# Dilated attention and a mixture of experts on one Trainium2 core: three matmuls of zeros at the start, and a straight run over all tile slots with the check at the end

## The chip, the cores and the metric

The kernel runs on one core of one Trainium2 chip. The core has a matrix engine (TensorE: PE, with its weight loads shown as PEld), a vector engine (VectorE: DVE), a scalar engine (ScalarE: ACT), GpSimd (POOL) and SyncE (SP), which issues most of the DMA transfers. The metric is device microseconds (us) of one execution; lower is better. A program is measured several times, and the median is given.

## The reference

The input is a batch of 8 sequences of 576 positions with 8 heads of 64 features. The first four heads attend to a window of 32 positions, the other four to every fourth position of a window of 128. The result, 4608 tokens of 512 features, goes to a layer of 8 experts in which every token has exactly one expert, its own best one or the one of the token before it:

```python
logits = np.einsum('bsd,de->bse', x, w_gate)
local_gate = 1.0 / (1.0 + np.exp(-np.einsum('bsd,de->bse', x, w_local).squeeze(-1)))
for b in range(B):
    prev_e = -1
    for s in range(S):
        fresh_e = int(np.argmax(logits[b, s]))
        if s == 0 or local_gate[b, s] < 0.5:
            e = fresh_e
        else:
            e = prev_e if prev_e >= 0 else fresh_e
        prev_e = e
        p = softmax(logits[b, s])
        h = np.maximum(x[b, s] @ w1[e], 0.0)
        out[b, s] = p[e] * (h @ w2[e])
```

`w1[e]` is 512 x 1024 and `w2[e]` is 1024 x 512. Everything is float32.

## The kernel before

`whole` holds the computation. It is called once with `exact=False`, and under a branch a second time with `exact=True`. In the fast version the exponentials of the attention are taken without subtracting a maximum, so a check of the sums of exponentials is needed: `check` (L683) tests whether all reciprocals of sums, kept in `rec`, lie within bounds, adds the answers up with one matmul over the partitions (`all`, L692), and writes one integer, `bad` (L693). If it is set, the branch at L168 runs the exact version over the same inputs. Both versions stand in the program; with these inputs only the fast one is executed.

**The attention stage.** The loop at L625 runs over 32 units of two heads. For each unit, `load` (L211) issues on SP the transfers of `kq` (592 KB) and `vt` (438.8 KB), two units ahead; `kq` has two buffers, `vt` three. `scores` (L250) makes 18 small matmuls into `sc` (36 instructions in the trace, since every float32 matmul appears there as two), DVE applies the mask (L266), ACT takes the exponential (L269), `values` (L302) multiplies by `vt` into `pv`, and after every second unit `turn` (L321) transposes the result with 128x128 matmuls (L332). Between the units the routing of finished quarters of the batch is fed in piece by piece by `gap` (L614): logits, choice of the expert, and `place` (L458), which scatters one row of a table `tab` in DRAM for each token with twelve indirect DMAs of GpSimd.

**The tile slots.** The tokens are grouped by expert into tiles of 128. With 4608 tokens and 8 experts there can be at most NT = 43 tiles; how many are really filled depends on the inputs. The kernel has 43 slots, numbered t. A slot without tokens has expert 7 (the number is clamped), the token number 4608, whose row in `xd` is zero, and for the output an address outside of `out_dram`, which the scatter drops. `expert(t)` (L661) is one slot:

- `hidden` (L589), twice: 32 instructions each on PE (L596), the rectifier on ACT (L598);
- `weights(t + 2, ...)` (L565): SP loads the expert's number into a register and issues the transfer of `w1s` (2048 KB) and later of `w2s` (2048 KB), with the condition that the expert differs from the one two slots before, since there are two buffers of each;
- `features(t + 1)` (L581): four transposes on PE (L585) and a copy on DVE (L587), one for each slot;
- `gather(t + 3)` (L574): two indirect DMAs of GpSimd;
- `output` (L600): 16 instructions on PE (L604), scaling on DVE (L606), scatter on GpSimd (L607).

**What sets the order.** PE runs in the order in which the program text issues its work (`manual_schedule`); the other engines' order is left to the framework. All matmul results share four PSUM banks (`bank`, L199). Slots 0 to 39 (LAST = 40) stand in line. After slot 18, `check` is issued, and its answer is loaded into a register of every engine (`register`, L680). After slot 36, `number`, the count of filled tiles that `table(True)` wrote at L513, is loaded in the same way. Slots 40 to 42 stand behind a branch on that number (L703), and then comes the branch on `bad` (L168):

```python
for t in range(LAST):
    expert(t)
    if t == CAP // 2 and not exact:
        again = check()
    if t == CAP:
        number = register(tiles["number"], NT, "a sum of tiles")
with tc.If(number > LAST):
    for t in range(LAST, NT):
        expert(t)
```

Of the kernel before, what the change touches and what calls it, by code (L numbers as in the profile page):

```python
# [10 lines left out]
F32 = mybir.dt.float32  # L11
BF16 = mybir.dt.bfloat16
I32 = mybir.dt.int32
U16 = mybir.dt.uint16
Act = mybir.ActivationFunctionType
Alu = mybir.AluOpType
# [6 lines left out]
P = 128  # L23
B, H, S, DH = 8, 8, 576, 64
D = H * DH
E, F = 8, 1024
# [33 lines left out]
CAP = N // P  # L60
NT = CAP + E - 1
# [6 lines left out]
EARLY, FIRST = 2, 11  # L68

KEPT = EARLY * GB * 2  # L70
assert EARLY * GS - E * (P - 1) > (FIRST - 1) * P

LAST = CAP + E // 2


FRESH = -(2.0 ** -23)
# [66 lines left out]
@with_exitstack  # L143
def dilated_attn_locality_moe_kernel(
    ctx: ExitStack,
    tc: tile.TileContext,
    qk: bass.AP,
    v: bass.AP,
    wgl: bass.AP,
    w1: bass.AP,  # L150
    w2: bass.AP,
    con: bass.AP,
    msk: bass.AP,
    qmk: bass.AP,
    out: bass.AP,
):
    nc = tc.nc
    keep = ctx.enter_context(tc.tile_pool(name="keep", bufs=1))
    cst = keep.tile([P, C_ALL], F32, name="cst")
    wg = keep.tile([P, DK, LW], F32, name="wg")  # L160
    ones = keep.tile([P, P], F32, name="ones")
    bad = keep.tile([1, 1], I32, name="bad")
    nc.vector.memset(ones, 1.0)

    args = (qk, v, wgl, w1, w2, con, msk, qmk, out, cst, wg, ones)
    again = whole(tc, False, bad, *args)

    with tc.If(again > 0):  # L168
        whole(tc, True, bad, *args)

# [2 lines left out]
def whole(ctx, tc, exact, bad, qk, v, wgl, w1, w2, con, msk, qmk, out, cst, wg, ones):  # L173
    nc = tc.nc
    name = "exact" if exact else "plain"
# [3 lines left out]
    def pool(name, bufs, **kw):  # L179
        return ctx.enter_context(tc.tile_pool(name=name, bufs=bufs, **kw))  # L180
# [7 lines left out]
    once = pool("once", 1)  # L188
# [10 lines left out]
    def bank(shape, name):  # L199
        return banks.tile(shape, F32, name=name, tag="bank")  # L200
# [10 lines left out]
    def load(n):  # L211
        kq = ins.tile([P, WIN + 2 * S], F32, name="kq", bufs=2)
        vt = ins.tile([KW, 2, NB, VW], F32, name="vt")
        nc.sync.dma_start(out=kq, in_=qk[n])
        nc.sync.dma_start(out=vt.rearrange("p u i e -> p (u i e)"), in_=v[n])
        loaded[n] = kq[:, :WIN + S], kq[:, WIN + S:], vt

    load(0)
    if not exact:
        mk = once.tile([KW, 2 * S], BF16, name="mk")  # L220
# [262 lines left out]
    tiles, stage = {}, {False: once}  # L483

    def table(late):
        nt = NT - FIRST if late else FIRST
        w = "late" if late else "early"

        def new(shape, name, dtype=F32):
            return stage[late].tile(shape, dtype, name=f"{name}_{w}")  # L490

        cn = bank([P, E], "cn")
        nc.tensor.matmul(cn, lhsT=ones[:TB], rhs=routes[NG - 1 if late else EARLY - 1]["cum"][:, :, NJ],
                         start=True, stop=True)
        ni = new([P, E], "ni", I32)
        nc.vector.tensor_scalar(ni, cn, float(P - 1) if late else 0.0, None, Alu.add)
        nc.vector.tensor_scalar(ni, ni, 7, None, Alu.logical_shift_right)
        nf = new([P, E], "nf")
        nc.vector.tensor_copy(nf, ni)
        if late:  # L500
            nc.vector.tensor_tensor(nf, nf, tiles["done"], op=Alu.subtract)
        end = new([P, E], "end")
        nc.vector.tensor_tensor_scan(end, nf, nf, 0.0, Alu.add, Alu.max)
        if not late:

            done = new([P, E], "done")
            nc.vector.tensor_tensor(done, nf, end, op=Alu.subtract)
            nc.vector.tensor_scalar(done, done, float(FIRST), 0.0, Alu.add, Alu.max)
            nc.vector.tensor_tensor(done, done, nf, op=Alu.min)
            tiles["done"] = done  # L510
        else:
            tiles["number"] = new([1, 1], "number", I32)
            nc.vector.tensor_scalar(tiles["number"], end[0:1, E - 1:], float(FIRST), None, Alu.add)  # L513
        ge = new([1, nt, E], "ge")
        shape = [1, nt, E]
        nc.vector.tensor_tensor(ge, end[0:1].unsqueeze(1).to_broadcast(shape),
                                cst[0:1, C_ROW:C_ROW + nt].unsqueeze(2).to_broadcast(shape), op=Alu.is_le)
        er = new([1, nt], "er")
        nc.vector.tensor_reduce(er, ge, axis=AX.X, op=Alu.add)
        tiles["experts", late] = experts = new([1, nt], "experts", I32)  # L520
        nc.vector.tensor_scalar(experts, er, float(E - 1), None, Alu.min)

        gc = new([nt, E], "gc")
        nc.vector.tensor_scalar(gc, end[:nt], cst[:nt, C_COL:C_PAY], None, Alu.is_le)
        ec = new([nt, 1], "ec")
        nc.vector.tensor_reduce(ec, gc, axis=AX.X, op=Alu.add)
        nc.vector.tensor_tensor(gc, gc, end[:nt], op=Alu.mult)
        at = new([nt, 1], "start")
        nc.vector.tensor_reduce(at, gc, axis=AX.X, op=Alu.max)
        nc.vector.tensor_tensor(at, cst[:nt, C_COL:C_PAY], at, op=Alu.subtract)  # L530
        nc.vector.scalar_tensor_tensor(at, ec, float(CAP), at, Alu.mult, Alu.add)
        if late:
            of = new([nt, E], "of")
            nc.vector.tensor_scalar(of, cst[:nt, C_IDX:C_REV], ec, None, Alu.is_equal)
            nc.vector.tensor_tensor(of, of, tiles["done"][:nt], op=Alu.mult)
            nc.vector.tensor_reduce(ec, of, axis=AX.X, op=Alu.add)
            nc.vector.tensor_tensor(at, at, ec, op=Alu.add)
        ri = new([nt, 1], "ri", I32)
        nc.vector.tensor_scalar(ri, at, float(PADS), None, Alu.min)
        tiles["rows", late] = tr = new([nt, P, TW], "tr")  # L540
        i = nc.gpsimd.indirect_dma_start(
            out=tr.rearrange("t s c -> t (s c)"), out_offset=None, in_=tab.rearrange("(r s) c -> r (s c)", s=P),
            in_offset=bass.IndirectOffsetOnAxis(ap=ri, axis=0))
        for s in scatters:
            tc.add_manual_dep(i.ins, s.ins.name, SYNC, reason="all places")
        table_users.append(i)
# [34 lines left out]
    def features(t):  # L581
        x = xg.pop(t).rearrange("p g f -> p (g f)")
        tp = bank([P, DK, P], "tp")
        for kk in range(DK):
            nc.tensor.transpose(tp[:, kk], x[:, kk * P:(kk + 1) * P], ident)  # L585
        xe[t] = mp.tile([P, DK, P], F32, name="xe")
        nc.vector.tensor_copy(xe[t], tp)  # L587
# [26 lines left out]
    def gap():  # L614
        if waiting:
            waiting.pop(0)()
# [41 lines left out]
        weights(t, True)  # L658

    features(0)  # L660
    def expert(t):  # L661
        if t == FIRST - 3:
            assert not waiting
            tokens(True)
        hidden(t, 0)
        gap()
        hidden(t, 1)
        gap()
        if t + 2 < NT:
            weights(t + 2, False)  # L670
        if t + 1 < NT:
            features(t + 1)
        if t + 3 < NT:
            gather(t + 3)
        output(t)
        gap()
        if t + 2 < NT:
            weights(t + 2, True)

    def register(value, most, why):  # L680
        return nc.values_load(value, min_val=0, max_val=most, skip_runtime_bounds_check_because=why)  # L681

    def check():  # L683

        flat = rec.rearrange("p n i -> p (n i)")
        fine = once.tile([P, NPB * NB], F32, name="fine")
        nc.vector.tensor_scalar(fine, flat, 1.0 / HIGH, None, Alu.is_ge)
        nc.vector.scalar_tensor_tensor(fine, flat, 1.0 / LOW, fine, Alu.is_le, Alu.mult)
        least = once.tile([P, 1], F32, name="least")
        nc.vector.tensor_reduce(least, fine, axis=AX.X, op=Alu.add)  # L690
        lp = bank([1, 1], "all")
        nc.tensor.matmul(lp, lhsT=least, rhs=ones[:, 0:1], start=True, stop=True)  # L692
        nc.vector.tensor_scalar(bad, lp, float(P * NPB * NB), None, Alu.is_lt)  # L693
        return register(bad[0:1, 0:1], 1, "a comparison's result")

    again = None
    for t in range(LAST):
        expert(t)
        if t == CAP // 2 and not exact:
            again = check()  # L700
        if t == CAP:
            number = register(tiles["number"], NT, "a sum of tiles")
    with tc.If(number > LAST):  # L703
        for t in range(LAST, NT):
            expert(t)
    return again

# [48 lines left out]
```

## Time before and its profile

| | |
|---|---|
| median of 3 runs | 842.93 us (841.5 to 846.79) |
| the profiled execution | 846.79 us, of which the trace's span is 845.0 us |
| PE busy (share of the span) | 776.0 us (92%), 6000 instructions |
| PEld busy | 593.9 us (70%) |
| DVE, ACT, POOL busy | 167.1 us, 117.5 us, 171.3 us |
| DMA | 179.60 MB, mean 213 GB/s |
| first instruction of L596, last scatter (L607) issued | 238.2 us, 830.5 us |

The page of a profile gives the busy time of each engine, the span in 40 equal slices with the busy share of each engine in tenths (here one slice is 21.1 us), the groups of instructions by line with their count, their total and mean duration and the idle time before them, and what ended that idle time. "PEclk" is the clock that TensorE was granted, in tenths of full speed. The timeline lists instructions in order of time, with adjacent ones of one kind merged; "idle before <-releaser" tells how long the engine sat idle before it, and what ended that. A "q" behind an engine's name means its sequencer, which handles registers, branches, semaphores and the issue of DMAs.

### The profile page before, as it was taken

How to read it: one execution, taken by the hardware profiler on the slowest of the kernel's cores; microseconds unless marked ns; L12 is line 12 of the kernel's file. 1: busy time of each engine (PE TensorE's matmuls, PEld its weight loads, DVE VectorE, ACT ScalarE, POOL GpSimd, SP SyncE). 2: the span in 40 equal slices, each digit the busy share in tenths (PEclk: the TensorE clock that was granted, in tenths of full speed). 3: DMA queues.
4: the chain of work that ended last, by engine and by line, in shares of the span. 5: the costliest groups of instructions: out<-in, count | busy, mean ns of one | idle time of the engine just before them, and what ended most of it. 6: DMA issues, size and time to landing. Idle time of an engine off the chain costs nothing. (4 is left out here: it accounts for less than half of the span.)

```text
span 845.0 us, 14238 instructions
## 1 busy us (share of the span) xinstructions
PE 776.0 (92%) x6000; PEld 593.9 (70%) x6000; DVE 167.1 (20%) x450; ACT 117.5 (14%) x201; POOL 171.3 (20%) x184
## 2 busy tenths in 40 slices
PE   6899698796779899999999999999999999999992
PEld 6878677675567577768686776768686767777770
DVE  3445254253312211110111111110011111111110
ACT  2342232232200000100000000101000000001010
POOL 1001303204042531121212121111212121212110
PEclk9985595578689999999999999999999999999997
DMA  8996685688948698989656571688118484282110
GB/s 284 254 260 183 133 253 141 186 263 227 318 140 304 195 365 322 332 318 330 243 211 251 192 279 38 236 321 327 40 38 310 152 295 171 70 324 104 35 39 16
DMA packets 44557, 179.60 MB, mean 213 GB/s; under 512 B 6403, under 2 KB 24963, under 8 KB 37568
## 3 DMA queue, kind: packets, MB, share of 16 engines
q1 hardware_dynamic: 35312, 157.06, 56.3%
q0 software_dynamic: 9168, 21.48, 7.4%
q8 instruction: 52, 0.85, 0.4%
q14 instruction: 25, 0.20, 0.1%
HBM read 230.28 MB, written 20.59 MB: 297 GB/s over the span
## 5 line engine op out<-in xcount | busy, mean ns | idle before, releaser
L596 PEld LDWEIGHTS hp<-xe,w1s 128*128 128x128 f32 x2560 | 294.2, 193 | 20.0 <-issue 17.9
L596 PE MATMUL hp<-xe,w1s 128*128 128x128 f32 x2560 | 295.5, 276 | 2.7 <-DVE bad L693 1.5
L604 PE MATMUL yp<-w2s,h 128*128 128x512 f32 x640 | 283.2, 595 | 3.9 <-issue 3.9
L604 PEld LDWEIGHTS yp<-w2s,h 128*128 128x128 f32 x640 | 119.0, 191 | 139.3 <-issue 139.3
L598 ACT ACTIVATE h<-hp 128x512 f32<-128x512 f32 x80 | 47.8, 597 | 541.6 <-PE hp L596 528.5
L261 PE MATMUL sc<-kq 64*96 64x64 f32 x1152 | 81.2, 308 | 17.0 <-issue 8.3
L261 PEld LDWEIGHTS sc<-kq 64*96 64x96 f32 x1152 | 75.5, 218 | 24.9 <-issue 14.1
L577 POOL DMA_INDIRECT xg<-xd,tok x43 | 41.8, 973 | 228.6 <-PE tp L585 150.7
L607 POOL DMA_INDIRECT out_dram<-y,tok x40 | 40.3, 1007 | 230.5 <-DVE y L606 193.4
L587 DVE COPY xe<-tp 128x512 f32<-128x512 f32 x41 | 28.3, 691 | 267.9 <-PE tp L585 259.8
L474 POOL DMA_INDIRECT tab<-cst,pi x48 | 44.0, 917 | 173.4 <-DVE pi L472 113.4
L606 DVE TENSOR_SCALAR y<-yp,gate 128x512 f32<-128x512 f32 x40 | 30.0, 751 | 244.9 <-PE yp L604 244.9
L312 PE MATMUL pv<-vt,pr 96*64 96x65 f32 x1152 | 62.7, 282 | 15.6 <-issue 15.6
L266 DVE SCALAR_TENSOR_TENSOR pr<-sc,mk 96x640 f32<-96x640 f32 x64 | 48.1, 753 | 114.3 <-PE sc L261 43.1
L312 PEld LDWEIGHTS pv<-vt,pr 96*64 96x64 f32 x1152 | 55.8, 191 | 20.2 <-issue 17.7
L269 ACT ACTIVATE pr<-pr 96x640 f32<-96x640 f32 x64 | 43.6, 684 | 132.0 <-DVE pr L266 127.8
L577 POOL DMA_INDIRECT xg<-xd,pos x43 | 40.8, 950 | 13.1 <-issue 11.9
L332 PE MATMUL tp<-cst,x 128*128 128x128 f32 x144 | 30.9, 379 | 5.9 <-issue 2.8
L332 PEld LDWEIGHTS tp<-cst,x 128*128 128x128 f32 x144 | 24.0, 197 | 9.3 <-issue 4.0
L585 PE MATMUL tp<-cst,xg 128*128 128x128 f32 x164 | 25.4, 277 | 3.8 <-DMA xg<-xd,tok 3.8
L317 DVE TENSOR_TENSOR x<-pv,rec 128x320 f32<-128x320 f32 x64 | 26.1, 447 | 0.1
L335 ACT COPY xt<-tp 128x384 f32<-128x384 f32 x48 | 22.9, 500 | 19.5 <-PE tp L332 10.4
(120 smaller groups left out, 111.6 us busy)
## 6 DMA issues: line engine op xcount, KB each, us to landing
w1s<-in_w_dram SPq DMA_DIRECT2D x44, 2048.0 KB
w2s<-in_w_dram SPq DMA_DIRECT2D x44, 2048.0 KB
kq<-in_qk_dram SPq DMA_DIRECT2D x32, 592.0 KB
vt<-in_v_dram SPq DMA_DIRECT2D x32, 438.8 KB
xd<-x SPq DMA_DIRECT2D x32, 288.0 KB
tab<-cst,pi POOLq DMA_INDIRECT x48
xg<-xd,tok POOLq DMA_INDIRECT x43
xg<-xd,pos POOLq DMA_INDIRECT x43
```

The costliest lines, as they stand in the source:

```text
L261: nc.tensor.matmul(sc[:KW, u, (i - a) * QB:(i - a + 1) * QB], lhsT=kt[h, i * QB:i * QB + KW], rhs=qt[h, i * QB:(i + 1) * QB], start=True, ...
L266: nc.vector.scalar_tensor_tensor(pr[:, :, :w], sc[:KW, :, :w], -CEIL, mk[:, at:at + w].unsqueeze(1).to_broadcast([KW, 2, w]), Alu.max, Alu ...
L269: nc.scalar.activation(pr[:, :, :w], pr[:, :, :w], Act.Exp, scale=SCALE)
L312: nc.tensor.matmul(pv[u * QB:(u + 1) * QB, i - a], lhsT=pr[:, u, (i - a) * QB:(i - a + 1) * QB], rhs=vt[:, u, i], start=True, stop=True, t ...
L332: nc.tensor.transpose(tp[:, i].rearrange("p u q -> p (u q)"), x[:, c * w + i].rearrange("p g d -> p (g d)"), ident)
L474: i = nc.gpsimd.indirect_dma_start(out=tab, out_offset=bass.IndirectOffsetOnAxis(ap=pi[:, j:j + 1], axis=0), in_=pay[:, g, j], in_offset=None)
L577: nc.gpsimd.indirect_dma_start(out=x[:, g], out_offset=None, in_=xd[g] if t >= FIRST else xd[g][:EARLY * GS], in_offset=bass.IndirectOffse ...
L596: nc.tensor.matmul(hp[:, m], lhsT=w1s[t % 2][:, half * FK // 2 + m, kk], rhs=x[:, kk], start=(kk == 0), stop=(kk == DK - 1))
L598: nc.scalar.activation(ht[t][:, half * FK // 2:(half + 1) * FK // 2], hp, Act.Relu)
L604: nc.tensor.matmul(yp, lhsT=h[:, m], rhs=w2s[t % 2][:, m], start=(m == 0), stop=(m == FK - 1))
L606: nc.vector.tensor_scalar(y, yp, of_tile("gate", t), None, Alu.mult)
L607: nc.gpsimd.indirect_dma_start(out=out, out_offset=bass.IndirectOffsetOnAxis(ap=of_tile("tok", t), axis=0), in_=y, in_offset=None, bounds_ ...
```

## The change

Four things are edited. Before the first load, DVE writes zeros into a tile `blank` of 128x512, and three matmuls of it with itself (128x128 by 128x512, float32) go into a PSUM bank `idle` that nobody reads. The branch at L703, the constant LAST, and the count `number` (L513 and its register loads) are gone: the loop runs over all 43 slots. The check is issued after the last slot in place of after slot 18. And the register load of `bad` stands in the calling function, behind all of it. The exact version has no check and no matmuls of zeros.

```diff
-    again = whole(tc, False, bad, *args)
+    whole(tc, False, bad, *args)
+    again = nc.values_load(bad[0:1, 0:1], min_val=0, max_val=1,
+                           skip_runtime_bounds_check_because="a comparison's result")
     with tc.If(again > 0):
         whole(tc, True, bad, *args)
...
+    if not exact:
+        blank = once.tile([P, 512], F32, name="blank")
+        nc.vector.memset(blank, 0.0)
+        idle = bank([P, 512], "idle")
+        for i in range(3):
+            nc.tensor.matmul(idle, lhsT=blank[:, :P], rhs=blank, start=True, stop=True, skip_group_check=True)
     load(0)
...
-        else:
-            tiles["number"] = new([1, 1], "number", I32)
-            nc.vector.tensor_scalar(tiles["number"], end[0:1, E - 1:], float(FIRST), None, Alu.add)
...
-    def expert(t):
+    for t in range(NT):
...
-    def check():
+    if not exact:
         flat = rec.rearrange("p n i -> p (n i)")
...
         nc.vector.tensor_scalar(bad, lp, float(P * NPB * NB), None, Alu.is_lt)
-        return register(bad[0:1, 0:1], 1, "a comparison's result")
-
-    again = None
-    for t in range(LAST):
-        expert(t)
-        if t == CAP // 2 and not exact:
-            again = check()
-        if t == CAP:
-            number = register(tiles["number"], NT, "a sum of tiles")
-    with tc.If(number > LAST):
-        for t in range(LAST, NT):
-            expert(t)
-    return again
```

On the engines: PE starts with the three matmuls and ends with slot 42, the matmul of the check and the register load of `bad`. DVE has the 128x512 memset third in its queue, ahead of the memsets of `fill`; its three large instructions of the check (L687 to L690) stay where they were, early in the program, and only the one that writes `bad` comes last, behind the scaling of slot 42. GpSimd issues 43 scatters in place of 40; the 43 pairs of gathers were issued before too.

## The prediction

> **What bounds the kernel now.** I read the page first, then the groups by line, then the timeline at each place that the change touches.
>
> ```profile
> span 845.0 us, 14238 instructions
> PE 776.0 (92%) x6000; PEld 593.9 (70%) x6000; DVE 167.1 (20%) x450; ACT 117.5 (14%) x201; POOL 171.3 (20%) x184
> PEclk9985595578689999999999999999999999999997
> DMA  8996685688948698989656571688118484282110
> L596 PE MATMUL hp<-xe,w1s 128*128 128x128 f32 x2560 | 295.5, 276 | 2.7 <-DVE bad L693 1.5
> L604 PE MATMUL yp<-w2s,h 128*128 128x512 f32 x640 | 283.2, 595 | 3.9 <-issue 3.9
> ```
>
> PE is the bound: 92% busy, and from about 290 us on at full clock almost without a gap. The counts matter most. A slot has 64 instructions of L596 and 16 of L604; 2560 / 64 = 40 and 640 / 16 = 40. So 40 slots were executed and the branch at L703 passed over slots 40 to 42: they are not in the 845.0 us.
>
> What is a slot worth? The copy of L587 occurs once in each slot, behind its transposes on PE, so its starts in the timeline of DVE are the clock of the loop:
>
> ```profile
> 517.28 0.69 DVE L587 COPY xe<-tp 128x512 f32<-128x512 f32 x1 [6.83 <-PE tp L585]
> 533.55 0.69 DVE L587 COPY xe<-tp 128x512 f32<-128x512 f32 x1 [8.59 <-PE tp L585]
> 548.00 0.69 DVE L587 COPY xe<-tp 128x512 f32<-128x512 f32 x1 [6.83 <-PE tp L585]
> ...
> 808.10 0.69 DVE L587 COPY xe<-tp 128x512 f32<-128x512 f32 x1 [6.83 <-PE tp L585]
> 822.55 0.69 DVE L587 COPY xe<-tp 128x512 f32<-128x512 f32 x1 [6.83 <-PE tp L585]
> ```
>
> The step is 14.45 us from 533.55 to the end (14.45 x 20 = 289.0 = 822.55 - 533.55). Only the step before it is 16.27 us, and there the check stands, as the timeline at 524 us shows:
>
> ```profile
> 524.04 0.19 PE L692 MATMUL all<-ones,least 128*1 128x1 f32 x2
> 524.82 0.14 DVE L693 TENSOR_SCALAR bad<-all 1x1 int32<-1x1 f32 x1
> 525.69 7.38 PE L596 MATMUL hp<-xe,w1s 128*128 128x128 f32 x64 [1.46 <-DVE bad L693]
> ```
>
> PE's queue holds the register load of `bad` ahead of slot 19, so it stood until DVE, behind the scaling of slot 18, had written the answer.
>
> The start, in the timeline of PE: 36 score matmuls take 3.14 us at first, and 1.75 us from 27.74 us on.
>
> ```profile
> 4.65 3.14 PE L261 MATMUL sc<-kq 64*96 64x64 f32 x36 [4.65 <-DMA kq<-in_qk_dram]
> ...
> 27.74 1.75 PE L261 MATMUL sc<-kq 64*96 64x64 f32 x36
> ...
> 36.57 1.89 PE L261 MATMUL sc<-kq 64*96 64x64 f32 x36 [1.37 <-DMA kq<-in_qk_dram]
> ```
>
> **What the Trainium skill says.** "TensorE: Matmul & The Clock Gate", section "What's actually happening": TensorE runs at half clock until it has been busy for a window of about 3.4 us, and falls back after an idle one. The trace agrees on the factor (3.14 against 1.75 us) but not on the time: PE was busy without a break from 15.18 to 27.74 us before the small score matmuls ran fast, and windows of 1 us over the first slot, whose full-width matmuls start at 236.05 us, show the clock rise at about 242.9 us, after 6.8 us.
>
> "Runtime: NRT & Kernel Launch", section "Instruction fetch mechanics": a taken branch to code that is not in the fetched pages waits for a fetch. The trace agrees: at L168, which jumps over the whole exact version, PE's branch took 3.34 us, and GpSimd's next instruction came 3.4 us after its branch. "VectorE: DVE Perf Modes", section "Zero memsets can be issued as uint32", gives one cycle per element for a memset; the trace has its own number, 1.02 us for 128x1152 (L232).
>
> **The change part by part.**
>
> *Three more slots.* Each has all the instructions of a filled one; that its tokens are missing takes none away. On PE, 3 x 14.45 = +43.35 us. Everything else lies beside that, as it does now: per slot 1.19 us of ACT, 1.44 us of DVE, 2.9 us of GpSimd. Would an empty slot wait for data? The gathers of slots 40 to 42 were issued already (43 pairs of L577 for 40 slots) and nothing waited. Its expert is 7; the last expert has five tiles, slots 35 to 39, so both weight buffers hold expert 7 by slot 36, and the conditional loads of slots 40 to 42 move nothing. DMA is nearly still in the last slices ("2110"). Without that cover: two matrices of 2048 KB at the 321 GB/s of the window from 360 to 400 us take 13 us, still less than a slot; a step of 15.56 us at 357 to 373 us shows what a tight load costs, +1.1 each, 3.3 for all. I take 43.35, with 42.5 to 46.7 as bounds.
>
> *The check out of the middle.* 16.27 - 14.45 = -1.82 us on PE. The three large DVE instructions stay early, off the path. The load of `number` on PE at 779.9 us goes too, worth nothing: the steps around it are 14.45. Next after the wait comes slot 19, whose data was there. `number`'s 0.14 us on DVE (L513) goes as well.
>
> *The end.* From the scaling of slot 39 (829.42) to the end are 15.6 us. GpSimd is last through it, as the lines for L703, L681, L168 and L754 show (min/median/max ns, first and last start):
>
> ```profile
> L703 POOLq INC_SWDGE_SEM  x1: 1395/1395/1395, 831.5 to 831.5; - x1
> L681 POOLq TENSOR_LOAD <-bad x1: 308/308/308, 832.9 to 832.9; - x1
> L168 POOLq COMPARE_BRANCH  x1: 45/45/45, 833.3 to 833.3; - x1
> L168 POOLq EVENT_SEMAPHORE  x5: 17/43/43, 836.7 to 837.1; - x5
> L168 POOLq INC_SWDGE_SEM  x1: 1367/1367/1367, 837.1 to 837.1; - x1
> L754 POOLq DRAIN  x3: 46/106/5118, 839.1 to 844.7; - x3
> ```
>
> Now GpSimd passes two branches, with a bookkeeping instruction of 1.40 us between them. After the change there is one. Counted from the scaling T: `bad` is written at T + 0.8 (as at 524.15 and 524.82); PE loads and branches by T + 1.4 and is through by T + 4.8; GpSimd issues the scatter at T + 1.0, loads `bad` meanwhile as it loaded `number` (830.6 = T + 1.2, 0.50 us), branches at T + 1.8, where it was at T + 3.9. So the check is ready before GpSimd asks, and the end shortens by 2.1 us; the drain of 5.1 us I leave. If the second bookkeeping instruction has to wait for the scatter that the first one awaited, or the drain hangs on something fixed, it shortens by nothing, and the late check can add its 0.8 us and a load of 0.5. Bounds -3.0 to +1.3; I take -2.1.
>
> *The zeros.* By 1.02 us x 512 / 1152, the memset takes 0.45 us; it stands behind `zero` (ends 1.27), so PE starts at about 2.0 us. Six instructions of 128x512: at half clock the weight loads at 287.5 to 290.1 us follow each other by 0.855 us, so 5.1 us, to 7.1 us. The first `kq` was there at 4.65. So the zeros aren't hidden: they hold the first scores up by up to 2.45 us. The third unit would come later by about 1.3, since the second waits for its `kq` until 8.9 anyway. If they wake the clock at about 6 us, the units until 27 us run fast, but only as far as `kq` arrives: DMA's idle share from 18 to 28 us adds up to 2.5 us, which is the gain. Then the clock falls back as it does at 38 us. Bounds +1.35 and -2.5; 5.1 us of zeros stand between the two warm-up times above, so I take 0. `fill`'s memset and its transfer come 0.45 us later, with nobody waiting; `idle` takes one bank of the rotation for a moment and is freed by PE's own order.
>
> *Sum.* 43.35 - 1.82 - 2.1 + 0 = +39.4 us. On the profiled execution: 846.79 (845.0 of span and 1.8 around it) + 39.4 = 886.2. That execution is the slowest of the three, 3.9 above the median; the steps are the same in any, so for the median 842.93 + 39.4 = **882.3 us**, 4.7% slower.
>
> **The rivals.**
>
> *Dearer slots or end.* The empty slots wait for weights (+3.3) or the moved check lengthens the end (+1.3 in place of -2.1, so +3.4): 882.3 + 3.4 = 885.7. For it: the end is the only place where a wait is added, and nothing runs beside it. Against it: DMA is still there, and GpSimd is later than the check. Chance 0.12.
>
> *The start shifts the attention stage.* The clock goes up and down four times before 240 us (the 5s to 8s in the row PEclk), so other timing at the start can move where it is up; one more or one fewer fast stretch of about 10 us, as from 27.7 to 38.4, is worth 4 to 5 us: 877 or 887. The spread of the three runs, 5.3 us, is of that size. Chance 0.13.
>
> *The other side: the clock stays up through the attention stage.* One mechanism: woken at the start, PE never falls to half clock before the slots begin. From 40 to 200 us the mean clock was 0.71, 0.67, 0.54 and 0.73 in windows of 40 us: 108 us at half clock, so 54 us of PE time at most; DMA's idle share in the same windows (0.17, 0.26, 0.38, 0.26) and at the start allows 47 us. Then 882.3 - 47 = 835. It decides only if L596 begins before about 199 us in place of 238. Against it: having risen by itself, the clock fell again after 11 us, at 38, with PE waiting for `kq`; fast scores wait more. Chance 0.02.
>
> *The change does not do what it says*, the slots being passed over in some other way: there is no branch left, so 0.01; it would give 839.
>
> The forecast itself has 0.72.
>
> **How the numbers follow.** The forecast's own range is 878.5 to 886.5: the start's -2.5 and +1.35, the end's bounds, and the spread of the runs (-1.4, +3.9) taken in part together. The first two rivals widen it to 876.5 to 888.5, with the last two and extreme sums of the bounds outside. What can be told from no change for this kernel is about 1%, 8 us: only the rival of 835 (within 1%, or just beyond it) and that of 839 come near. Slower 0.97, within 1% 0.02, faster 0.01.
>
> **What would show it.** In the profile after: 2752 instructions of L596's code and 688 of L604's (43 slots); steps of 14.45 us throughout, the last three too, and none of 16.27; full clock and still DMA over the last 43 us; PE's first matmuls at about 2 us and the first scores between 6 and 7.1; one bookkeeping instruction at the last branch, and about 13.5 us from the last scaling to the end, in place of 15.6. The first slot's matmuls near 238 us, within 5. I am wrong if empty slots take another time than filled ones, if weights move after slot 39, or if the first slot begins more than 8 us from 238.

## The result, and the profile after

The change makes the kernel slower, by somewhat less than the 43.35 us of three more slots. Measured first: 876.88 us (median of 4 executions, 872.61 to 882.5) against 842.21 us, ratio 1.0412 with a 95% interval of 1.0334 to 1.0490. Measured again with more executions of the kernel before (27) and six of the change: 882.19 against 842.28 us, ratio 1.0478 (1.0423 to 1.0533). The forecast was 882.3 on 842.93, a ratio of 1.0467.

The page of the kernel after, lines that answer to those shown of before:

```profile
span 870.8 us, 14754 instructions
PE 797.0 (92%) x6254; PEld 601.4 (69%) x6254; DVE 170.5 (20%) x455; ACT 119.6 (14%) x207; POOL 173.7 (20%) x187
PEclk8898695896899999999999999999999999999997
L600 PE MATMUL hp<-xe,w1s 128*128 128x128 f32 x2752 | 317.5, 276 | 1.2 <-issue 0.8
L608 PE MATMUL yp<-w2s,h 128*128 128x512 f32 x688 | 304.3, 595 | 3.9 <-issue 3.9
```

2752 / 64 = 43 and 688 / 16 = 43 slots, at the same mean durations as before (276 and 595 ns). The wait for `bad` in front of L596 is gone from L600's idle time.

The profiled execution took 872.61 us, only 25.8 more than that of before. The two are extremes: of the four executions of each kernel, the change's was the shortest and before's the longest. The DVE timeline tells where the difference lies. The fifth copy of the slots (L587 before, L591 after) starts at 299.42 us before and at 286.62 after: 12.8 us earlier, in a part of the program that the change hardly touches. From there to the end of the span it is 545.6 us before and 584.2 after: +38.6. In that part the steps are as forecast, to the last:

```profile
793.48 0.69 DVE L591 COPY xe<-tp 128x512 f32<-128x512 f32 x1 [6.83 <-PE tp L589]
807.93 0.69 DVE L591 COPY xe<-tp 128x512 f32<-128x512 f32 x1 [6.83 <-PE tp L589]
822.38 0.69 DVE L591 COPY xe<-tp 128x512 f32<-128x512 f32 x1 [6.83 <-PE tp L589]
836.83 0.69 DVE L591 COPY xe<-tp 128x512 f32<-128x512 f32 x1 [6.83 <-PE tp L589]
...
857.71 0.75 DVE L610 TENSOR_SCALAR y<-yp,gate 128x512 f32<-128x512 f32 x1 [13.26 <-PE yp L608]
858.38 0.14 DVE L694 TENSOR_SCALAR bad<-all 1x1 int32<-1x1 f32 x1
```

Steps of 14.45 us, for slots without tokens too; no step of 16.27 is left. (One step of 15.56 us, the ninth, stands in both kernels alike.) From the last scaling (857.71) to the end are 13.1 us, where it was 15.6. GpSimd's lines in the views of L166, L168 and L742 (min/median/max ns, first and last start):

```profile
L166 POOLq TENSOR_LOAD <-bad x1: 495/495/495, 858.6 to 858.6; - x1
L168 POOLq COMPARE_BRANCH  x1: 53/53/53, 859.1 to 859.1; - x1
L168 POOLq INC_SWDGE_SEM  x1: 1455/1455/1455, 863.3 to 863.3; - x1
L742 POOLq DRAIN  x3: 50/106/5213, 864.8 to 870.5; - x3
```

One branch and one bookkeeping instruction are left of two.

The start, in the timeline of PE:

```profile
1.87 4.34 PE L224 MATMUL idle<-blank 128*128 128x512 f32 x6 [1.87 <-DVE blank L221]
6.14 1.75 PE L268 MATMUL sc<-kq 64*96 64x64 f32 x36
9.22 1.75 PE L268 MATMUL sc<-kq 64*96 64x64 f32 x36 [1.33 <-DVE pr L273]
10.89 1.27 PE L319 MATMUL pv<-vt,pr 96*64 96x65 f32 x36
15.82 3.14 PE L268 MATMUL sc<-kq 64*96 64x64 f32 x36 [3.66 <-DMA kq<-in_qk_dram]
21.05 3.15 PE L268 MATMUL sc<-kq 64*96 64x64 f32 x36
```

The second to fourth unit before (the first, at 4.65, stands in the prediction):

```profile
8.90 3.15 PE L261 MATMUL sc<-kq 64*96 64x64 f32 x36 [1.11 <-DMA kq<-in_qk_dram]
15.18 3.15 PE L261 MATMUL sc<-kq 64*96 64x64 f32 x36 [0.98 <-DVE x L317]
20.40 3.15 PE L261 MATMUL sc<-kq 64*96 64x64 f32 x36
```

The zeros do wake the clock: the first two units take 1.75 us where they took 3.14. But then PE stands 3.66 us until the third `kq` arrives, and the third and fourth units take 3.14 and 3.15 us again. What was won is given back in that wait: the third unit starts no earlier than before, and neither does the fourth.

Single executions of the kernel before lie between 835.72 and 852.1 us (59 of one set), with no gap that would part fast from slow ones, and the ratios leave out what is over 1.5% above a kernel's fastest, so for differences of a few us the table below also gives the mean of all executions against the mean of all of before, with a bootstrap interval of 95%.

### The profile page after: what moved, and what is told of

Its sections match the earlier page's. It is cut to its first block, busy times and chain, and to the rows that moved or that the text cites. A ratio compares the mean times of both kernels' runs of the same rounds, so it can differ in the third digit from the quotient of the medians.

```text
span 870.8 us, 14754 instructions
## 1 busy us (share of the span) xinstructions
PE 797.0 (92%) x6254; PEld 601.4 (69%) x6254; DVE 170.5 (20%) x455; ACT 119.6 (14%) x207; POOL 173.7 (20%) x187
## 4 chain that ended last, share of the span: by engine, by line
PE 88%; issue 5%; DMA 3%; DVE 2%; POOL 0%; ACT 0%; POOLq 0%; DVEq 0%
PE hp L600 36%; PE yp L608 34%; PE sc L268 7%; PE pv L319 5%; DMA kq<-in_qk_dram 3%; PE tp L589 2%; PE tp L339 2%; PE lp L365 1%; DVE pr L273 1%; PE idle L224 0%; DMA xg<-xd,pos 0%; DVE x L324 0%; DVE rec L323 0%; DVE y L610 0%; PE kp L471 0%
## 5 line engine op out<-in xcount | busy, mean ns | idle before, releaser
L600 PEld LDWEIGHTS hp<-xe,w1s 128*128 128x128 f32 x2752 | 316.3, 193 | 20.4 <-issue 19.9
L600 PE MATMUL hp<-xe,w1s 128*128 128x128 f32 x2752 | 317.5, 276 | 1.2 <-issue 0.8
L608 PE MATMUL yp<-w2s,h 128*128 128x512 f32 x688 | 304.3, 595 | 3.9 <-issue 3.9
L608 PEld LDWEIGHTS yp<-w2s,h 128*128 128x128 f32 x688 | 127.9, 191 | 149.3 <-issue 149.3
L591 DVE COPY xe<-tp 128x512 f32<-128x512 f32 x43 | 29.7, 691 | 280.4 <-PE tp L589 265.3
L319 PE MATMUL pv<-vt,pr 96*64 96x65 f32 x1152 | 55.7, 251 | 26.3 <-issue 26.3
L268 PE MATMUL sc<-kq 64*96 64x64 f32 x1152 | 68.0, 277 | 12.7 <-DMA kq<-in_qk_dram 7.6
L268 PEld LDWEIGHTS sc<-kq 64*96 64x96 f32 x1152 | 63.0, 190 | 20.2 <-issue 14.4
L319 PEld LDWEIGHTS pv<-vt,pr 96*64 96x64 f32 x1152 | 48.1, 161 | 32.2 <-issue 30.0
L581 POOL DMA_INDIRECT xg<-xd,pos x43 | 40.7, 947 | 13.1 <-issue 11.9
L339 PE MATMUL tp<-cst,x 128*128 128x128 f32 x144 | 25.7, 324 | 5.1 <-issue 2.7
L589 PEld LDWEIGHTS tp<-cst,xg 128*128 128x128 f32 x172 | 20.2, 142 | 5.0 <-issue 3.7
```

The costliest lines, as they stand in the source:

```text
L268: nc.tensor.matmul(sc[:KW, u, (i - a) * QB:(i - a + 1) * QB], lhsT=kt[h, i * QB:i * QB + KW], rhs=qt[h, i * QB:(i + 1) * QB], start=True, ...
L319: nc.tensor.matmul(pv[u * QB:(u + 1) * QB, i - a], lhsT=pr[:, u, (i - a) * QB:(i - a + 1) * QB], rhs=vt[:, u, i], start=True, stop=True, t ...
L339: nc.tensor.transpose(tp[:, i].rearrange("p u q -> p (u q)"), x[:, c * w + i].rearrange("p g d -> p (g d)"), ident)
L581: nc.gpsimd.indirect_dma_start(out=x[:, g], out_offset=None, in_=xd[g] if t >= FIRST else xd[g][:EARLY * GS], in_offset=bass.IndirectOffse ...
L600: nc.tensor.matmul(hp[:, m], lhsT=w1s[t % 2][:, half * FK // 2 + m, kk], rhs=x[:, kk], start=(kk == 0), stop=(kk == DK - 1))
L608: nc.tensor.matmul(yp, lhsT=h[:, m], rhs=w2s[t % 2][:, m], start=(m == 0), stop=(m == FK - 1))
```

## The experiments

The question after the first measurement: the forecast was +39.4, and +34.7 was measured (medians), while the trace was 12.8 us ahead before the fifth slot. Are the zeros worth it after all, or is that spread? Rows with the same median of before were measured together, each such set on another chip, so rows of different sets are compared by their differences from before.

| kernel | median, before's median (us) | ratio (95%) | mean difference (us, 95%) |
|---|---|---|---|
| the change again | 882.19, 842.28 | 1.0478 (1.0423 to 1.0533) | +38.7 (35.4 to 41.9) |
| three zeros alone | 845.17, 842.28 | 1.0032 (1.0009 to 1.0056) | +3.1 (1.3 to 5.0) |
| the change without zeros | 883.22, 842.28 | 1.0448 (1.0379 to 1.0517) | +40.0 (35.0 to 44.9) |
| 43 slots, check in the middle | 882.48, 842.28 | 1.0487 (1.0429 to 1.0545) | +40.4 (37.4 to 43.3) |
| one zero matmul | 843.15, 843.46 | 0.9986 (0.9959 to 1.0013) | -0.1 (-2.2 to 1.9) |
| six zero matmuls | 845.1, 843.46 | 1.0019 (0.9994 to 1.0045) | +2.2 (-0.2 to 4.5) |
| float32 zeros in every unit | 857.86, 843.46 | 1.0193 (1.0146 to 1.0241) | +14.4 (11.4 to 17.4) |
| check last, branch kept | 843.97, 843.46 | 0.9932 (0.9904 to 0.9961) | -1.3 (-3.8 to 1.2) |
| bfloat16 zeros, one a unit | 846.2, 839.42 | 1.0053 (1.0026 to 1.0081) | +5.8 (3.3 to 8.1) |
| bfloat16 zeros, two a unit | 860.67, 839.42 | 1.0215 (1.0168 to 1.0262) | +19.1 (15.9 to 22.3) |

**The change again.** No edit.

> The whole change, measured again beside the next three. Slots, check and end were priced at +39.4 us together, with nothing for the zeros. Theory A (the zeros shift the clock in the attention stage and save some us): 36 us or less above the kernel before, and more than 3 us below the same without the zeros. Theory B (the zeros are worth nothing, the few us missing are spread between executions): the same as without the zeros, within 2 us.

**Three zeros alone**, in the kernel before:

```diff
+    if not exact:
+        blank = once.tile([P, 512], F32, name="blank")
+        nc.vector.memset(blank, 0.0)
+        idle = bank([P, 512], "idle")
+        for i in range(3):
+            nc.tensor.matmul(idle, lhsT=blank[:, :P], rhs=blank, start=True, stop=True, skip_group_check=True)
     load(0)
```

> The kernel before with the three matmuls of zeros at the start and nothing else. Theory A: 3 to 6 us below the kernel before (837 to 839), the clock in the attention stage higher than before's 0.71, 0.67, 0.54, 0.73 in windows of 40 us from 40 us on. Theory B: within 2 us of the kernel before.

**The change without zeros**: the same lines taken out of the kernel after.

> The change without its zeros: straight run over 43 slots, check at the end. The sum for slots, check and end is 43.35 - 1.82 - 2.1 = +39.4 us. Theory A: 39 to 40 us above the kernel before (about 881.6), and slower than the whole change by 3 to 6 us. Theory B: 34 to 36 us above, equal to the whole change. Theory C (the slots themselves or the end are cheaper than priced): also 34 to 36 us above, but then the time from the last scaling to the end or a slot's step is shorter than 13.5 us or 14.45 us.

Theory A falls: it asked for 3 to 6 us less than the kernel before, and the zeros alone made that kernel slower, by some 3 us. The change with and without them gives 882.19 and 883.22 us, but six executions of each can't tell a few us apart. Theory C falls as well: without zeros the steps are 14.45 us and the end takes 13.0 (from 869.00 to 882.0). Of theory B's "nothing", the 3 us remain to be explained. The start with three zeros alone, in the timeline of PE:

```profile
1.86 5.12 PE L224 MATMUL idle<-blank 128*128 128x512 f32 x6 [1.86 <-DVE blank L221]
6.91 1.75 PE L268 MATMUL sc<-kq 64*96 64x64 f32 x36
9.43 1.75 PE L268 MATMUL sc<-kq 64*96 64x64 f32 x36 [0.77 <-DMA kq<-in_qk_dram]
11.10 1.27 PE L319 MATMUL pv<-vt,pr 96*64 96x65 f32 x36
16.10 2.62 PE L268 MATMUL sc<-kq 64*96 64x64 f32 x36 [3.72 <-DMA kq<-in_qk_dram]
20.80 3.15 PE L268 MATMUL sc<-kq 64*96 64x64 f32 x36
```

It is the picture of the whole change: two fast units, a wait of 3.72 us for `kq`, and half clock from within the third unit on.

The traces show too where the 12.8 us of the first comparison belong. The first matmul of L596's code starts at 238.2 us before, at 225.3 and 224.2 in the two traces of the change, at 230.8 without its zeros, at 228.0 in the next kernel, and at 235.1 with zeros alone. Kernels without zeros are among the early ones and one with zeros is among the late ones. The straight run over the slots doesn't sort them either: three kernels further down that keep the branch begin at 228.7 to 231.4. The two traces of the change are also the shortest executions of their sets, 872.61 of four and 875.38 of six. From the fifth copy to the end, on the other hand, the three traces with straight slots and the check last have 584.2, 584.6 and 584.1 us, and the seven with the branch kept and the check in the middle 545.6 to 547.1. The spread is made before the fifth slot.

**43 slots, check in the middle.** The loop of the change in the kernel before, with the check where it was and no zeros:

```diff
-        else:
-            tiles["number"] = new([1, 1], "number", I32)
-            nc.vector.tensor_scalar(tiles["number"], end[0:1, E - 1:], float(FIRST), None, Alu.add)
...
-    for t in range(LAST):
+    for t in range(NT):
         expert(t)
         if t == CAP // 2 and not exact:
             again = check()
-        if t == CAP:
-            number = register(tiles["number"], NT, "a sum of tiles")
-    with tc.If(number > LAST):
-        for t in range(LAST, NT):
-            expert(t)
     return again
```

> The kernel before with the loop over all 43 slots and without the count and the branch at it; the check stays after slot 18, no zeros. By the steps of the prediction: +43.35 for the slots, the middle step stays at 16.27 us, and at the end one of the two bookkeeping instructions of GpSimd goes: -2.1, so +41.3 us, and 1.8 us slower than the kernel with the check at the end. If the check at the end costs what it cost in the middle, the two are equal.

The times are equal to the change's within their intervals, which are too wide to decide between 0 and the 1.8 us of the expectation; the trace separates the parts. The step at the check is 16.27 us, as in the kernel before:

```profile
513.19 0.69 DVE L584 COPY xe<-tp 128x512 f32<-128x512 f32 x1 [6.83 <-PE tp L582]
529.46 0.69 DVE L584 COPY xe<-tp 128x512 f32<-128x512 f32 x1 [8.60 <-PE tp L582]
```

From the last scaling (868.24 us) to the end (880.1) are 11.9 us, while the three traces with the check last have 13.1, 13.5 and 13.0. GpSimd's lines of L168:

```profile
L168 POOLq COMPARE_BRANCH  x1: 53/53/53, 869.6 to 869.6; - x1
L168 POOLq INC_SWDGE_SEM  x1: 1455/1455/1455, 872.6 to 872.6; - x1
```

GpSimd branches 1.4 us after the scaling in both, but gets on 3.0 us later here and 4.2 us later in the kernel after. So a late check is not free: about 1.2 us of its 1.82 come back at the end (1.1 to 1.6 over the three traces; this side is one trace). In the kernel after all five engines branch within 0.3 us (858.9 to 859.2); here SP, ACT and PE branched before GpSimd (840.2, 861.9, 862.0). The other traces fit this: in the four with the check last, SP, ACT and DVE branch within 0.4 us, and their next instructions come 3.1 to 4.5 us later; in the eight others ACT branches about 7 us or more before DVE, and it is 2.4 to 3.4 us. That the fetches of the jump's target get in each other's way is what this suggests; it was not tested alone.

**One zero matmul, and six.** `range(1)` and `range(6)` in place of `range(3)` in the kernel with zeros alone.

> The kernel before with one matmul of zeros at the start in place of three. It should be over at about 3.6 us, before the first kq lands. Theory D (the zeros cost what they hold the first scores up by): the same as before, within 1 us, where three zeros cost 2.7 us. Theory E (the cost is the memset, the PSUM bank or only spread): the same 2 to 3 us above before as with three.

> The kernel before with six matmuls of zeros. Half of them at half clock and half at full clock, they end at about 9.5 us, some 2.5 us later than three. Theory D: another 2 to 3 us on top of three zeros, so about 847. If the wait of the third unit for its kq (3.7 us with three zeros) swallows it: no more than three zeros, 845. A longer time awake gives nothing in either theory, since the clock falls in that same wait.

Starts of the two, in the timeline of PE, first one and then six:

```profile
1.87 2.08 PE L224 MATMUL idle<-blank 128*128 128x512 f32 x2 [1.87 <-DVE blank L221]
4.79 3.14 PE L268 MATMUL sc<-kq 64*96 64x64 f32 x36 [0.85 <-DMA kq<-in_qk_dram]
...
16.17 3.14 PE L268 MATMUL sc<-kq 64*96 64x64 f32 x36 [1.35 <-DMA kq<-in_qk_dram]
```

```profile
1.86 8.42 PE L224 MATMUL idle<-blank 128*128 128x512 f32 x12 [1.86 <-DVE blank L221]
10.22 1.75 PE L268 MATMUL sc<-kq 64*96 64x64 f32 x36
...
17.18 2.29 PE L268 MATMUL sc<-kq 64*96 64x64 f32 x36 [2.02 <-DMA kq<-in_qk_dram]
```

One zero matmul is over before the first `kq` and costs nothing that the interval shows, as theories B and D say; memset and bank are there too, so they are not what costs 3 us. But D falls with six: they hold the first scores up until 10.22 us and cost no more than three. The reason is in the third lines: the third unit starts when its `kq` is there, at 16.17, 16.10 and 17.18 us with one, three and six, though the first one started at 4.79, 6.91 and 10.22. By the fourth unit nothing is left of the delay: it starts at 20.80 to 21.65 us in four traces with three or six zeros, and at 20.40 to 21.81 in five with one or none. So the 3 us of three zeros are not the delay of the first scores handed on. Their interval only just leaves zero out, and that of six holds it; part or all of them can be spread, and where else they would arise stays open.

**Float32 zeros in every unit**, on top of the kernel with three zeros. This tests the prediction's rival in which the clock stays up through the attention stage.

```diff
             sc = scp.tile([P, 2, 512], F32, name="sc")
+            if a == 0:
+                nc.tensor.matmul(sc[:, 0], lhsT=blank[:, :P], rhs=blank, start=True, stop=True, skip_group_check=True)
             for i in range(a, z):
```

> The kernel before with three zeros at the start and one more matmul of zeros at the head of each unit of the attention stage, written into the sc tile that the unit's scores then overwrite. This tests the rival in which the clock stays up through the attention stage. PE gets 32 x 0.85 us = 27 us more work, beside waits for kq where there are any. If the full-width zeros keep the clock up, it is 0.95 or more in the windows from 40 to 200 us and the first slot begins at 200 us or before, so 810 or less. If the clock falls all the same (in the waits and in the stretches where PE issues hardly anything), the added work costs about its 27 us and more at half clock: 865 or more.

Neither half came out as written. Two windows (busy times and counts of PE, PEld, DVE, ACT and POOL, then the clock, the DMA share and GB/s), and two lines of PE's timeline between them:

```profile
40.00:80.00 40.00, 34.99 (x567) 25.31 (x565) 20.50 (x68) 13.01 (x24) 4.33 (x5) 1.00 0.87 245
80.00:120.00 40.00, 27.70 (x426) 19.51 (x426) 14.33 (x40) 11.33 (x21) 6.73 (x8) 0.83 0.58 166
```

```profile
76.73 1.07 PE L341 MATMUL tp<-cst,x 128*128 128x128 f32 x6
90.85 0.87 PE L341 MATMUL tp<-cst,x 128*128 128x128 f32 x3 [13.04 <-DVE rec L325]
```

The clock stays at 1.00 as long as units follow each other; all of them take 1.75 us until 90 us. It falls only in three long stops of PE, of 13.0, 13.1 and 13.9 us, each beside the twelve scatters that `place` issues on GpSimd. In the first, DVE and ACT do three instructions between them, from 80.3 to 81.6 us, and otherwise stand as well. The kernel before has stretches at the same places (86 to 97, 144 to 156, 203 to 217 us) in which up to 2.3 us pass between two matmuls of PE. So PE's clock is not what holds the stage there. Between the stops a fast clock is paid for by the zeros, which take 38 us of PE's busy time, and the first slot begins at 239.1 us. For the rival this means that a clock held up in this way doesn't end the stage early; what a fast clock would be worth that costs no work on PE, the run does not show.

**Bfloat16 zeros**, in the kernel before, without zeros at the start: the same insertion with a bfloat16 `blank`, once with `if a == 0` and once at the head of both `sc` tiles.

> The kernel before, no zeros at the start, but one bfloat16 matmul of zeros (128x128 by 128x512, a single instruction) at the head of each unit of the attention stage, into the sc tile that the scores then overwrite. The float32 zeros of the run before this kept the clock at 1.00 from 0 to 80 and from 160 to 200 us, but cost 32 x 1.0 us on PE[...]. Theory F (full-width work keeps the clock up, however short): clock 0.95 or more from 40 to 80 us, the units at 2.9 us plus 0.2, and some 10 to 20 us below the kernel before. Theory G (it takes as much full-width work as one float32 matmul a unit): the clock goes up and down as before, and the time is the same as before or up to 7 us above.

> The same with two such matmuls a unit, one at the head of each sc tile[...]. Theory F: the clock is up as well, and the time is about 7 us above that with one where PE sets the pace, or equal where kq does. Theory G: if the amount of full-width work counts, the clock is higher than with one a unit.

With one a unit, in windows:

```profile
40.00:80.00 40.00, 35.67 (x587) 29.06 (x585) 22.73 (x75) 14.64 (x26) 0.98 (x1) 0.87 0.85 244
120.00:160.00 40.00, 30.43 (x342) 25.62 (x338) 17.06 (x72) 9.29 (x16) 10.95 (x12) 0.55 0.60 162
```

And with two:

```profile
40.00:80.00 40.00, 36.99 (x590) 28.30 (x589) 20.62 (x64) 14.44 (x27) 0.00 (x0) 0.91 0.85 246
160.00:200.00 40.00, 38.31 (x480) 29.33 (x478) 17.53 (x55) 12.82 (x23) 0.35 (x1) 0.71 0.68 225
```

Theory F falls: the clock goes up and down as without zeros, and with one a unit the time is 3 to 8 us above before. Whether two raise the clock, as theory G allows, is not shown: its mean over the four windows from 40 to 200 us is 0.81, with one 0.74, and the nine traces without zeros in the units lie between 0.66 and 0.82. Only the float32 zeros, with 0.905, stand above these, in one trace. What the bfloat16 zeros cost on PE can be read: with the clock up, PE's next instruction starts 0.31 us after one (28.38 and 28.69 us in the trace with one a unit). By this figure I estimate 20 us for the 64 of two a unit, close to the 19.1 us on the mean.

**Check last, branch kept:**

```diff
-    again = None
     for t in range(LAST):
         expert(t)
-        if t == CAP // 2 and not exact:
-            again = check()
...
         for t in range(LAST, NT):
             expert(t)
+    again = None if exact else check()
     return again
```

> The kernel before with the check moved from behind slot 18 to behind the branch over the last three slots, nothing else. The step of 16.27 us becomes 14.45, -1.82 us; at the end the answer of the check is needed behind GpSimd's first bookkeeping instruction, which takes longer than the check, so nothing comes back there: 840.5, at most 2 us below before. If the check costs at the end what it did in the middle: the same as before.

In its trace no step of 16.27 us is left, and the end is 17.2 us long (825.08 to 842.3). The seven traces with the old end have 15.6 to 17.1 us, 16.4 on the mean, so some of what is won in the middle may come back here, but one trace so near the others does not show it. The time can't tell the two expectations apart either. The medians are nearly equal, the mean of all executions is 1.3 us lower with an interval that holds both 0 and -1.8, and the ratio of 0.9932 is no gain: a very short execution (830.87 us) makes it rest on ten of the 22.

None of these versions is shown to beat the kernel before.

## Why the prediction was right

**The slots: right.** 40 to 43 slots, 14.45 us each, nothing waiting, and DMA's share of the windows' time was 0.06 from 780 to 857 us. One term was overlooked: slot 42 has no successor, so its transposes are missing, while slot 39 still made those of slot 40. The stretch from the last copy to the last scaling is 6.87 us before and 20.88 = 14.45 + 6.43 after: -0.44 us. With it the trace adds up: 43.35 - 0.44 (transposes) - 1.82 (check) - 2.49 (end, 15.58 to 13.09) = 38.6, what the two traces differ by behind the fifth copy. From the mean of seven old ends, 16.4 us, to that of the three new ones, 13.2, it would be 37.9.

**The check out of the middle: right**, 1.82 us, shown by the step of 16.27 that stays when the check stays and goes when it goes.

**The end: near in sum, wrong in its parts.** -2.1 was forecast, -2.5 came in this pair. GpSimd branches 1.4 us after the last scaling in place of 3.9, somewhat earlier than the 1.8 of the forecast. It branches as early when the check is in the middle, so the late check does not hold it up there, but it is not free for that: without it the end is 11.9 us. The branch was worth more than forecast and the late check costs about 1.2 us of it. The 15.6 of before is itself the shortest of seven old ends; from their mean, 16.4, to the 13.2 of the three new ones are -3.2, a little outside of the bound of -3.0. That the pair lay so near the forecast is partly luck.

**The zeros: no gain, as priced, but a cost beyond the bounds.** Taken as 0, they measured +3.1 (1.3 to 5.0) by themselves. The first scores began behind them at 6.1 to 7.3 us, as worked out. The gain of "up to 2.5 us" failed because the clock does not last until 27 us: it falls in the wait for the third `kq`, which the faster start makes longer. The cost bound of +1.35 came from handing the first delay on, and the runs show that it is gone by the fourth unit; the measured 3.1 lies mostly above the bound and is not explained.

**The spread: too small.** The three executions known then spanned 5.3 us; 59 span 16.4. The first median of the change, 876.88, lay below the forecast's own range (from 878.5) and only 0.4 us inside the widened one; repeated, it was 882.19, so its low value is best read as spread and not as something that the change does better. That 882.19 lies within 0.1 us of the forecast is luck, with intervals of several us and terms that were off both ways: the zeros cost about 3 us more than priced, end and transposes about 1.5 less. One of the prediction's own signs of being wrong did come: the first slot began 12.7 and 13.8 us before 238 in the two traces of the change, where 8 was the limit. The 238 of one trace was no fixed mark, since the kernels without zeros in the units spread from 224 to 238. The rival in which the start shifts the attention stage was thus seen in single traces, but with and without zeros alike, so no edit here is shown to cause it.

**The rival on the other side** was refuted as a consequence of the three zeros: the clock is down again by the third unit, at about 16 us. Holding it up with more zeros did not help either; the first slot then began at 239.1, with 38 us of zeros on PE.

## What to carry to other kernels

Count instructions first: 2560 and 640 matmuls said that the last slots were not executed, and a periodic instruction gave their price to the hundredth of a microsecond. Waking the clock before the data arrive was worth nothing here, because the data behind the first ones did not keep up; and a matmul of zeros stands in the queue ahead of the real one, so look at the arrival of the third transfer and not only of the first. When a difference sits in a part that the change does not touch, repeat the measurement before looking for its cause.

## What the runs showed of the hardware

- The granted clock from 40 to 80 us and from 160 to 200 us was 1.00 in both windows with one float32 zero matmul (two instructions of 128x512) in each unit of 64- and 96-row matmuls. In nine traces without zeros in the units it was 0.71 to 0.99 and 0.71 to 0.93, and one or two bfloat16 zero matmuls a unit (0.87 and 0.81; 0.91 and 0.71) can't be told from these.
- Three float32 matmuls of zeros took 4.3 to 5.5 us over four traces. Their instructions, 0.85 us apart at first, became fast at different moments: the first one of 0.59 us started at 5.19 us in one trace, at 5.95 in another, and with six matmuls at 7.98.
- The profile gives a clock of 0.98 for the first 40 us of the kernel before, although its units take 3.14 us until 27 us and 1.75 after that. For the start, go by the durations.
- A jump over the exact version cost GpSimd 2.7 to 4.2 us until its next instruction, over twelve traces.
- While GpSimd issued twelve scatters of table rows, PE stood for 13 us, and DVE and ACT for most of that. What stops them was not studied here.
